# Loading k and v with transposing loads of 256 columns in place of 128, under another written-out order

## The chip, the cores and the metric

The kernel runs on one core of one Trainium2 chip. The metric is the device time of one execution in microseconds (us). Executions can fall into a slower state, so only fast ones are compared. Every execution of the changed kernel and of the variants was of the fast state; of the kernel before, two were slow (318.95 and 317.03 us, in the rounds of e1 to e4 and of e9 to e11) and are left out of every ratio. The one run of e8, another program, is of unknown state. "Times" below are these device times; a profile's "span", from the first to the last instruction, is about 1.7 us shorter.

## The reference

A block with conditioning by six modulation vectors, one sequence of S = 2048 positions, D = 640 channels, bf16:

```python
def _A_ref(q, k, v, shift_k, ssm_k, ssm_D):
    # k_shift: 4-tap causal convolution of k, one filter for each channel
    for t in range(ks):
        k_shift = k_shift + k_pad[:, t:t + S, :] * shift_k[:, ks - 1 - t][None, None, :]
    kv = k_shift * v
    # ... FFT convolution of kv with ssm_k along the sequence (length 2 S) ...
    y = y + kv * ssm_D[None, None, :]
    return q * y
# ...
mod = (_silu(c) @ w_mod).reshape(c.shape[0], 6, 1, -1)       # sa, ca, ga, sb, cb, gb
h = _layernorm(x, axis=-1) * (1 + ca) + sa
x = x + ga * _A_ref(h, A_k, A_v, A_shift_k, A_ssm_k, A_ssm_D)
h = _layernorm(x, axis=-1) * (1 + cb) + sb
x = x + gb * _B_ref(h, B_w1, B_w2, B_w3, B_w4)               # LayerNorm, w1, gelu, shifts, w2, LayerNorm, w3, gelu, w4
```

So k and v are needed early, with channels on the partitions: k is shifted, multiplied with v, and goes into the FFT. The LayerNorms and the four weight matrices of the second part come late.

## The kernel before

Every piece of work is a task with a number. A task knows on which engine it may run, what it reads and writes, and which slots it takes in PSUM, the memory that PE's matmuls write to. The order is not computed: it is written out as a string of task numbers, each with the letter of its engine (S, P, D, A, G for SP, PE, DVE, ACT, POOL) and its PSUM places, and is replayed. Each engine executes its tasks strictly in that order.

```python
CODE = {"P": "PE", "A": "ACT", "D": "DVE", "G": "POOL", "S": "SP"}

def run(self):
    order, seen = [], set()
    for word in ORDER.split():
        head, _, places = word.partition(":")
        t = self.tasks[int(head[:-1])]
        t.on = self.CODE[head[-1]]
        # ... asserts: engine allowed, all dependencies earlier ...
        for sl, place in zip(t.alloc, places):
            sl.place = place
        seen.add(t)
        order.append(t)
    return order
```

The loads that change. A block is 128 channels; there are ND = 5:

```python
for b in range(ND):
    for dst, off, src, key in ((kT, 16, k_flat, "kT"), (vT, 0, v_flat, "vT")):
        add("SP", 3.0, lambda e, b=b, dst=dst, off=off, src=src:
                nc.sync.dma_start_transpose(dst[:, b, off:off + S], src[:, b * P:(b + 1) * P]),
            w=[(key, b, b + 1)], kb=524, rate=200.0)
```

Their users, twice for each block (half a sequence each): PE shifts k by matmuls with diagonal matrices (L456), DVE multiplies with v (L461).

```python
def k_shift(b, s2):
    # PE: four taps, two 512-column halves, into one PSUM slot
    nc.tensor.matmul(pt[:, i, :], lhsT=diagw[:, b, jj, :], rhs=kT[:, b, c0:c0 + 512], start=(jj == 0), stop=(jj == 3))
    # ...
    # DVE: v times the shifted k, in place of v
    nc.vector.tensor_tensor(vs, ps.tile[:].rearrange("p i n -> p (i n)"), vs, ALU.mult)
```

Three late pieces matter to the argument. The statistics of the first LayerNorm, one task of about 1.1 us on DVE for each of 16 tiles (L521 and L522), feed a small finishing task on POOL (L527 to L530):

```python
def ln1_stats(A):
    for i in range(2):
        nc.vector.bn_stats(st[:, i, :], x_all[:, A, i * 320:(i + 1) * 320])
    nc.vector.bn_aggr(mv1[:, A, :], st[:])
```

The other LayerNorms end in `ln_finish`, on DVE or POOL (L667 to L669) and then on POOL (L674 to L676); then `norm` (L557 on ACT, L559 on DVE) scales a tile. And `turn` brings a normalised tile to the transposed form that w1 needs: by PE (L722) and a copy (L728 or L730) for the first three of eight pairs of tiles, by a transposing DMA between two SBUF tiles (L715) for the other five:

```python
pe_tr = (0, 1, 2)

def turn(dT, dk, src, sk, i, g):
    if g not in pe_tr:
        add("SP", 1.3, lambda e: nc.sync.dma_start_transpose(dT[:, :, i * P:(i + 1) * P], src), r=[sk], w=[dk + ("t",)], lat=1.6)
        return
    # ... else five PE transposes into a PSUM slot, then a copy by ACT or DVE ...
```

## Time and profile before

| | kernel before |
|---|---|
| time, median of the 3 runs known at the prediction | 314.69 us (313.75 to 314.99) |
| span of the profiled run | 311.9 us |
| PE, DVE, ACT, POOL busy | 88%, 73%, 63%, 33% |
| bound to some 110 us | DVE (busy 9.3 to 9.9 of each 10 us in 40 to 80 us) and the DMA engines (mean share 0.81 to 1.13 there) |
| bound from some 155 us | PE (busy 29.9 to 30.0 of each 30 us in 170 to 290 us) |

The lines themselves stand in the prediction, with what is to be seen in each. To read them: in a timeline row the first number is the start in us, the second the busy time (for SPq: the time that the issue held SP's queue), then engine, line, operation, output and inputs, and the count of instructions merged in the row. Brackets at the end, where there are any, give the engine's idle time before the row and what ended it.

### The profile page before, as it was taken

What the parts mean: (1) busy time and instruction counts of PE and PEld (TensorE: products, weight loads), DVE (VectorE), ACT (ScalarE), POOL (GpSimd) and SP (SyncE); (2) the same over time, 40 slices, a digit from 0 to 9 for tenths busy, and PEclk for the clock granted to TensorE, in tenths of its full rate; (3) what the DMA queues carried; (4) which work ended last, traced back from release to release, by engine and by line L of the source; (5) the groups of instructions that cost most, each with busy time, mean ns of one, the idle gap of its engine ahead of it and who ended that gap; (6) DMA issues with size and microseconds to landing.
All of it is one profiled execution on the core that took longest, in us unless ns stands there. A gap on an engine that the chain in (4) does not pass through costs nothing.

```text
span 311.9 us, 7129 instructions
## 1 busy us (share of the span) xinstructions
PE 275.1 (88%) x2816; PEld 204.7 (66%) x2816; DVE 228.1 (73%) x460; ACT 197.3 (63%) x314; POOL 101.8 (33%) x227
## 2 busy tenths in 40 slices
PE   0998999999688844778799999999999999999993
PEld 0655656655588632556588787778886768878762
DVE  8999999999999999888976687758744245124233
ACT  4788997889377869879647566766694604342100
POOL 4888227005211416763434331223312103010000
PEclk9999999999789965579999999999999999999998
DMA  5998999997999700820055020221224110320111
GB/s 179 293 184 196 224 182 210 274 226 184 238 253 233 194 9 8 299 92 2 1 128 191 2 58 2 53 49 22 58 61 55 40 41 16 76 53 22 33 47 51
DMA packets 56817, 35.39 MB, mean 113 GB/s; under 512 B 38528, under 2 KB 53504, under 8 KB 56784
## 3 DMA queue, kind: packets, MB, share of 16 engines
q1 hardware_dynamic: 55552, 31.49, 42.6%
q0 software_dynamic: 1136, 3.41, 4.4%
q8 instruction: 22, 0.36, 0.5%
q14 instruction: 11, 0.09, 0.1%
q10 hardware_dynamic: 96, 0.04, 0.1%
HBM read 16.31 MB, written 2.62 MB: 61 GB/s over the span
## 4 chain that ended last, share of the span: by engine, by line
PE 59%; DVE 19%; ACT 8%; POOL 4%; issue 4%; DMA 3%; SPq 0%; DVEq 0%; ACTq 0%; POOLq 0%
PE ps_w L876 18%; PE ps_w L857 17%; PE ps_w L824 5%; DVE Rb L582 5%; PE ps_w L769 4%; PE ps_ksh L456 4%; ACT R L208 3%; PE ps_s L407 2%; PE ps_s L424 2%; DMA Ra<-in_A_ssm_k_dram 2%; PE ps_mod L482 2%; DMA RH<-in_w_mod_dram 2%; DVE R L704 2%; DVE Rb L394 2%; DVE R L461 1%
## 5 line engine op out<-in xcount | busy, mean ns | idle before, releaser
L857 PE MATMUL ps_w<-R,T 128*128 128x256 bf16 x560 | 63.5, 273 | 0.5 <-ACT R L728 0.4
L857 PEld LDWEIGHTS <-T 128*128 128x128 bf16 x560 | 54.4, 98 | 8.3 <-issue 1.6
L876 PE MATMUL ps_w<-T,R 128*128 128x320 bf16 x416 | 59.0, 299 | 0.0
L876 PEld LDWEIGHTS <-R 128*128 128x128 bf16 x416 | 40.6, 98 | 15.4 <-issue 0.3
L861 ACT ACTIVATE R<-ps_w 128x1024 bf16<-128x1024 f32 (+1 forms) x32 | 28.5, 910 | 26.9 <-PE ps_w L857 26.9
L681 ACT ACTIVATE RG<-R 128x640 bf16<-128x640 bf16 x32 | 23.5, 735 | 24.9 <-DVE R L832 18.2
L899 DVE TENSOR_TENSOR T<-ps_w,R 128x640 bf16<-128x640 f32 x15 | 12.3, 823 | 33.6 <-PE ps_w L876 17.2
L208 ACT CAST T<-ps_s 128x1024 bf16<-128x1024 f32 x33 | 31.8, 1018 | 7.4 <-PE ps_s L407 7.2
L407 PE MATMUL ps_s<-F1bd,Rb 128*128 128x256 bf16 x160 | 23.0, 292 | 9.1 <-DVE Rb L394 8.4
L208 ACT CAST R<-ps_s 128x640 bf16<-128x640 f32 x42 | 26.8, 724 | 2.7 <-PE ps_s L424 2.4
L407 PEld LDWEIGHTS <-Rb 128*128 128x128 bf16 x160 | 16.4, 104 | 15.6 <-DVE Rb L394 9.0
L824 PE MATMUL ps_w<-RG,R 128*128 128x320 bf16 x160 | 23.4, 299 | 1.5 <-ACT R L771 1.4
L594 PE MATMUL ps_i<-EB,Rb 128*128 128x128 bf16 x160 | 21.8, 236 | 2.7 <-DVE Rb L582 2.7
L674 POOL TENSOR_TENSOR lnv<-stat,lnv 128x2 f32<-128x2 f32 x24 | 7.0, 290 | 51.7 <-ACT RG L681 44.9
L593 PE MATMUL ps_i<-EA,Rb 128*128 128x128 bf16 x160 | 21.9, 235 | 1.9 <-DVE Rb L582 1.6
L208 ACT CAST T<-ps_i 128x1024 bf16<-128x1024 f32 x18 | 17.2, 1026 | 9.1 <-PE ps_i L594 8.4
L424 PE MATMUL ps_s<-T,RG 64*128 64x320 bf16 x256 | 21.8, 297 | 0.8 <-ACT R L208 0.3
L769 PE MATMUL ps_w<-R,RG 128*128 128x256 bf16 x160 | 21.7, 299 | 0.0
L824 PEld LDWEIGHTS <-R 128*128 128x128 bf16 x160 | 15.2, 98 | 8.1 <-ACT R L771 2.3
L675 POOL TENSOR_TENSOR lnv<-lnv,mhalf 128x2 f32<-128x2 f32 x24 | 19.4, 810 | 1.9
L594 PEld LDWEIGHTS <-Rb 128*128 128x128 bf16 x160 | 16.9, 107 | 4.8 <-DVE Rb L582 4.4
L769 PEld LDWEIGHTS <-RG 128*128 128x128 bf16 x160 | 17.2, 108 | 3.7 <-issue 0.3
(156 smaller groups left out, 502.6 us busy)
## 6 DMA issues: line engine op xcount, KB each, us to landing
RH<-in_w_mod_dram SPq DMA_DIRECT2D x8, 400.0 KB, 5.3
Ra<-in_A_ssm_k_dram SPq DMA_DIRECT2D x5, 512.0 KB, 6.2
Ra<-in_A_q_dram SPq DMA_DIRECT2D x8, 320.0 KB, 6.2
out_dram<-RH SPq DMA_DIRECT2D x60, 40.0 KB, 1.6
T<-in_B_w_dram SPq DMA_DIRECT2D x1, 2160.0 KB, 8.3
T<-in_B_w_dram SPq DMA_DIRECT2D x1, 2080.0 KB, 9.8
RK<-in_w_mod_dram SPq DMA_DIRECT2D x4, 400.0 KB, 4.8
RK<-R SPq DMA_DIRECT2D x5, 256.0 KB, 5.2
```

Source lines behind the costliest of these rows:

```text
L208: nc.scalar.copy(dst, src(ps.tile))
L407: nc.tensor.matmul(psv[:, ml, :], lhsT=xL[:, s0:s0 + P], rhs=F1r, start=True, stop=True)
L424: nc.tensor.matmul(psv[:, g], lhsT=Gs[p, k, 64 - 64 * cc:192 - 64 * cc], rhs=T1b[p, cc * 32 + k], start=(cc == 0), stop=(cc == 1), tile_po ...
L593: nc.tensor.matmul(psv[:, w, :], lhsT=Av[:, r_, :, g_], rhs=EAf, start=True, stop=False)
L594: nc.tensor.matmul(psv[:, w, :], lhsT=Bv[:, r_, :, g_], rhs=EBf, start=False, stop=True)
L675: nc.gpsimd.tensor_tensor(rs, rs, mhalf[:, 0:n], ALU.pow)
L681: add("ACT", 0.74, lambda e: nc.scalar.activation(junk, src, ACT.Square, scale=float(D) ** -0.5, accum_out=stat[:, li, 1, t:t + 1]), r=[sk ...
L769: nc.tensor.matmul(pt[:, fb, :], lhsT=w1_sb[:, b, 160 * fb:160 * fb + P], rhs=hT[:, b, :], start=(b == 0), stop=(b == ND - 1))
L824: nc.tensor.matmul(pt[:, hf, 0:320], lhsT=gsf[:, fb, c0:c0 + P], rhs=w2_sb[:, fb, 320 * hf:320 * hf + 320], start=(fb == 0), stop=(fb == 4))
L857: nc.tensor.matmul(pt[:, fl, :], lhsT=w3_sb[:, b, fb * P:(fb + 1) * P], rhs=xT[:, b, :], start=(b == 0), stop=(b == ND - 1))
L861: nc.scalar.activation(g3[g % 2][:, f0:f0 + fn, :], ps.tile[:, 0:fn, :], ACT.Gelu_apprx_tanh)
L876: nc.tensor.matmul(pts[i][hf][:, hf, 0:320], lhsT=gg[:, fb, i * P:(i + 1) * P], rhs=w4_sb[:, fb, 320 * hf:320 * hf + 320], start=(fb == 0 ...
```

## The change

The intent is fewer and larger loads: four of 1 MiB and two of 512 KiB in place of ten of 512 KiB. The order was written anew to fit (1051 tasks in place of 1055), for the whole kernel, not for its beginning alone.

```diff
 ORDER = """
-19G 0S 18D 20D 21G 23D 22D 24A 56G 27G 29D 28D 25A 2S 31A 30A 36G 37G 68G 69D 26G 90P:0 91A 86P:1 6S 87A 88P:2 89A 4S 72G 73D 104P:3 105A 102P:0
... (the whole string is replaced) ...
+0S 2S 15G 14D 16D 17G 18D 21A 6S 23G 25D 24D 3S 64D 26A 19D 65D 20A 27A 32G 33G 34G 35D 22G 84P:0 36A 5S 85A 82P:1 83A 66G 52G 4S 70G 80P:2 81A 67D
... (the whole string is replaced) ...
 """
@@
-    for b in range(ND):
+    for b, n in ((0, 2), (2, 2), (4, 1)):
         for dst, off, src, key in ((kT, 16, k_flat, "kT"), (vT, 0, v_flat, "vT")):
-            add("SP", 3.0, lambda e, b=b, dst=dst, off=off, src=src: nc.sync.dma_start_transpose(dst[:, b, off:off + S], src[:, b * P:(b + 1) * P]),
-                w=[(key, b, b + 1)], kb=524, rate=200.0)
+            add("SP", 3.0, lambda e, b=b, n=n, dst=dst, off=off, src=src: nc.sync.dma_start_transpose(dst[:, b:b + n, off:off + S], src[:, b * P:(b + n) * P]),
+                w=[(key, b, b + n)], kb=524 * n, rate=200.0)
```

More of the change, by code (lines that the diff above doesn't have):

```diff
@@ L26 @@
 ORDER = """
-19G 0S 18D 20D 21G 23D 22D 24A 56G 27G 29D 28D 25A 2S 31A 30A 36G 37G 68G 69D 26G 90P:0 91A 86P:1 6S 87A 88P:2 89A 4S 72G 73D 104P:3 105A 102P:0
-106P:1 107A 38G 39G 40A 3S 70D 71D 96P:2 97A 98P:3 103D 99A 5S 74G 75D 49G 1S 66G 94P:0 50G 8S 118P:1 9S 114P:2 115A 10S 92P:3 93A 95D 41G 52D 51D 32D
-53A 116P:0 110P:2 119D 84P:3 42G 11S 43G 34S 7S 54A 33G 44A 85A 111A 67D 117D 122P:1 123D 112P:3 113A 108P:2 109A 100P:0 101D 76P:3 77A 203S 45G 47S
-46S 78P:1 79D 35S 82P:2 83A 80P:0 81A 120P:3 170P:1 283D 121D 178P:2 55G 171A 176P:0 179A 180P:1 177A 65G 181D 194P:3 198P:2 195A 199D 234S 48S 202S
@@ L31 @@
-148P:0 57G 58G 200S 149A 142P:1 201S 143D 182P:3 183A 140P:2 141D 231S 12S 13S 144P:0 145A 188P:1 14S 136P:3 15S 189A 137D 162P:2 163A 156P:0 157D
-164P:1 165A 150P:3 151D 190P:2 191A 168P:0 174P:1 175A 169D 196P:3 197A 138P:2 139D 160P:0 161A 16S 186P:1 158P:3 159A 146P:2 184P:0 185A 187D 17S
-166P:1 167A 147D 192P:3 193A 235P:2 236A 152P:0 213D 232P:1 153A 233A 208D 154P:3 155A 172P:2 288P:0 173A 294P:1 295A 289A 284D 126P:3 298P:2 302P:1
-209D 124P:0 214D 59G 60A 299A 303A 210D 296P:2 297A 130P:1 300P:2 301A 127D 125D 290P:3 291A 128P:0 61G 211D 62G 63G 64A 237S 285D 304P:2 306P:3 307A
@@ L35 @@
-131D 134P:1 129D 286D 305A 310P:0 311A 215G 132P:3 312P:2 313A 135D 133D 238P:0 239D 292P:1 293A 314P:3 315A 316P:2 287D 243S 244P:0 245D 240S 318P:1
-317D 319A 326P:3 327D 320P:0 321A 324P:1 325A 322P:2 308P:0 241P:3 212G 393G 246S 247P:1 309A 323D 352P:2 353A 348P:0 242D 248D 486D 380P:3 381A 349D
-252S 253P:1 254D 330P:2 331A 346P:0 347D 338P:3 339A 356P:1 357A 334P:2 335D 392S 390P:0 391A 354P:3 355D 376P:1 362P:2 489D 205S 350P:0 351D 377A
-249S 250P:3 251D 363A 261S 487D 366P:1 367A 255S 382P:2 383D 332P:0 333A 340P:3 341A 262P:1 263A 217D 258S 344P:0 342P:2 343A 328P:3 329A 256P:1 345D
@@ L39 @@
-257D 374P:2 375A 480D 358P:0 276S 359D 364P:3 365A 388P:1 389A 259P:2 260A 275G 281S 481D 279G 277G 264S 368P:0 278G 282G 280G 272S 386P:3 273G 270S
-268S 271G 274G 490D 384P:1 387A 385A 360P:2 369D 378P:0 379A 269S 361D 372P:3 373A 336P:1 370P:2 371A 267S 265P:0 492A 216D 337D 401G 266A 400S 394D
-395D 408S 409G 396P:3 398P:2 399A 493D 491D 402D 494D 397A 403D 410D 404P:1 405A 411D 406P:0 418D 412P:2 413A 417G 414P:3 415A 416S 419D 426D 422P:1
-423A 424S 420P:2 421A 425G 427D 434D 433G 407A 432S 435D 430P:3 431A 428P:1 442D 441G 438P:2 436P:0 437A 440S 443D 446P:3 444P:0 450D 448S 449G 451D
@@ L43 @@
-447A 456S 439A 429A 454P:3 457G 458D 483A 459D 464S 452P:2 466D 460P:1 445A 462P:0 453A 465G 467D 206S 455A 463D 470P:2 471D 461A 207S 468P:3 469A
-488D 495P:01 496A 497A 498P:23 500A 482D 479G 474S 484D 485D 204S 220D 226D 219D 519D 520D 508P:01 218G 499A 543D 522D 523D 524A 544D 477S 525G 521A
-510A 526G 557D 554D 472S 555D 558D 560D 475S 501G 602D 559A 502P:32 509A 556A 545D 546D 503A 531D 527D 532D 528D 504A 529D 530A 561G 533D 535D 511P:10
-534A 505P:32 603D 605D 606D 547D 512A 536G 566A 540D 541P:1 513A 537D 538P:0 562A 563D 542A 539D 478G 221G 564D 551P:1 567D 607A 604A 608G 506A 609G
@@ L47 @@
-568D 565A 569A 570D 552A 610D 611D 517S 612D 571G 572D 575D 549P:0 550A 553G 476S 573P:3 574D 613A 514S 576P:1 577D 586P:0 614D 615D 616D 618D 617A
-619G 587A 584P:3 585A 578D 579D 507A 580D 548D 672D 623D 624P:1 625A 620D 621P:0 622A 473S 591P:3 634P:2 588P:1 675D 676D 677A 673D 678D 592D 674A
-679G 593A 635A 589D 590A 684D 632P:0 518G 633A 636P:3 685D 594G 686D 687A 581D 680D 681D 682D 683A 595G 599D 600P:1 596D 637D 601D 638A 597P:2 639P:0
-598A 656P:3 657A 650P:1 688D 582D 640D 641A 689G 225D 583D 516S 223D 690A 652P:2 691S 740D 642G 643G 644D 692D 693S 647D 648P:0 649D 653A 654P:3 626D
@@ L51 @@
-627D 651A 645P:0 628D 743D 744D 745A 702P:2 700P:1 703A 701A 646D 724P:0 720P:2 741D 742A 227G 746G 704P:1 655A 222D 224G 694D 629D 721A 747G 748D
-695D 229D 705D 707P:3 725A 718P:2 515S 658P:01 630D 708D 709A 749D 706A 710G 711G 631D 715D 712D 752D 719A 753D 754D 750D 756G 755A 806D 660D 716P:3
-717D 713P:2 714A 228D 659P 661D 663S 790P:2 722P:0 786P:3 666D 751A 757G 760A 758A 791A 230G 828D 829D 788P:1 761S 696D 809D 810D 807D 723A 812D 811A
-808A 813G 818D 814A 787A 819D 726P:20 759S 770P:3 815D 816D 697D 789A 728D 768P:1 771A 765D 820D 821A 817A 769A 784P:2 766D 664S 822D 698D 699D 823G
@@ L55 @@
-824A 826D 665S 827S 825S 767D 729D 775P:3 776D 777A 785A 772P:1 773D 778G 774A 667D 727P 833P:3 834A 730S 779G 732S 782A 831P:1 869D 870D 929D 662S
-734D 735D 832A 871A 780D 781S 762A 763D 792P:20 764D 872D 873D 669S 838P:3 737S 839D 731S 874A 739S 830D 835P:1 836D 840A 783S 853P:3 854A 794D 837A
-841D 851P:1 849P:2 793P 847P:3 875G 876G 877D 881A 882D 842G 843A 845A 883D 844S 846S 930D 931A 878D 879D 880A 885G 733S 884A 668S 932D 933D 935D 886G
-887A 888S 850A 800D 801D 802S 907P:0 934A 936G 848A 852A 913P:2 909P:3 941A 889D 908A 942D 943D 671S 944A 890S 893P:1 894A 738S 891P:0 937D 938D 939D
@@ L59 @@
-940A 945D 946G 911P:1 914A 947D 803S 892A 898P:2 899D 910A 948S 949D 950S 670S 895P:0 896D 900A 897A 901D 902G 795D 804S 796S 855P:32 857D 951P:0 952A
-799S 953P:3 798S 856P 863D 736S 858D 954A 959P:0 805S 960D 956P:3 905A 906S 955G 990P:2 991D 993P:0 994D 862S 1041D 912A 915P:12 917D 918D 903A 904S
-974P:0 968P:1 957D 958A 961A 970P:3 969A 797S 864D 865S 972P:1 916P 975A 992A 866S 922S 973A 962G 963G 964D 965S 966D 923D 967S 1004P:0 1005A 995A
-971A 1002P:1 1003A 1006P:2 1007A 861S 976P:03 920S 996G 997G 921S 868S 919S 867S 998D 999S 1000A 978D 1042D 1008P:1 1009A 859S 860S 924D 977P 984D
@@ L63 @@
-1001S 1028P:2 1029A 1030P:0 985D 989S 926S 1024P:1 1031A 987S 1010P:32 986S 988S 979D 983S 980S 1026P:0 925S 927S 1012D 1025A 928S 1013D 1016S 1011P
-1018D 982S 1014S 981S 1019D 1021S 1020S 1023S 1027A 1032P:130 1022S 1035D 1036D 1017S 1015S 1040S 1037S 1033P 1043D 1039S 1044D 1048S 1047S 1038S
-1045S 1034P 1049D 1050D 1053S 1052A 1046S 1051S 1054A
+0S 2S 15G 14D 16D 17G 18D 21A 6S 23G 25D 24D 3S 64D 26A 19D 65D 20A 27A 32G 33G 34G 35D 22G 84P:0 36A 5S 85A 82P:1 83A 66G 52G 4S 70G 80P:2 81A 67D
@@ new lines @@
+94P:3 1S 71D 95A 45G 8S 88P:0 89A 110P:1 68G 111A 69D 108P:2 109D 104P:3 46G 47D 105A 106P:0 107A 9S 86P:1 87D 28D 30S 92P:2 93A 29S 90P:3 91D 98P:0
+37G 38G 39G 40A 41D 43S 42S 100P:1 101A 99A 49A 62G 227S 48D 31G 44S 63D 198S 7S 196S 197S 199S 112P:2 113D 102P:3 96P:1 97A 114P:0 115D 72P:1 103A
+50A 73A 74P:2 230S 75A 78P:3 79D 76P:0 279D 77A 118P:1 119D 176P:2 164P:3 51G 165A 116P:0 117D 177A 188P:3 189A 136P:1 137A 162P:2 163D 170P:3 10S
+171A 172P:0 61G 173D 152P:1 153A 178P:2 179A 150P:3 151D 146P:0 156P:1 157D 147A 154P:2 155A 138P:3 139D 158P:0 166P:1 159A 167D 142P:2 143A 192P:3
@@ new lines @@
+140P:0 190P:1 141A 11S 191A 193D 186P:2 187D 194P:3 195A 180P:0 181D 144P:1 145A 148P:2 149D 134P:3 135A 182P:0 174P:1 184P:2 53G 175A 183A 280D
+231P:3 232A 228P:1 185D 132P:0 229A 133A 160P:3 161D 168P:1 169A 294P:2 295A 209D 389G 207D 54G 292P:0 293A 55G 288P:3 289A 206D 12S 205D 296P:1 297A
+120P:2 210D 290P:0 291A 284P:3 122P:1 204D 285A 13S 123D 56A 239S 121D 298P:0 299A 126P:3 127D 57G 58G 286P:1 124P:0 59G 60A 128P:2 287A 281D 300P:3
+208G 301A 125D 306P:1 307A 129D 130P:0 282D 304P:3 305A 302P:2 303A 233S 234P:1 131D 235D 308P:3 309A 283D 312P:0 313D 314P:2 315A 310P:1 311A 240P:3
@@ new lines @@
+241D 201S 316P:2 317A 318P:1 319A 322P:0 320P:3 321A 323D 482A 236S 237P:2 238D 242S 243P:1 248S 244D 485D 348P:0 349A 386P:2 376P:3 377A 387D 249P:1
+250D 344P:0 372P:2 373D 211G 345A 388S 352P:3 353A 334P:1 335D 350P:0 330P:2 331D 351A 358P:3 359A 342P:1 488D 245S 246P:0 247D 343A 326P:2 327A
+346P:3 347D 328P:1 329A 362P:0 363A 368P:2 369D 324P:3 257S 258P:1 325A 340P:0 213D 251S 259D 254S 336P:2 271S 275G 277S 341A 337A 252P:3 253D 489D
+274G 360P:0 378P:1 361A 260S 278S 370P:2 371A 338P:3 379D 486D 255P:0 264S 263G 256D 339A 476D 267G 366P:2 367A 268S 332P:1 333D 382P:3 265G 266S 269S
@@ new lines @@
+383A 364P:0 365D 270G 380P:2 381A 276S 212D 374P:1 375A 354P:3 355A 272G 384P:2 385A 273S 356P:0 261P:1 262A 357D 390D 391D 396S 397G 404S 394P:3 490D
+477D 483D 392P:2 405G 398D 399D 402P:0 403A 406D 400P:1 395A 407D 410P:0 408P:3 393A 411A 414D 413G 412S 415D 418P:2 422D 419A 401A 416P:0 417A 420S
+421G 423D 424P:2 425A 426P:1 427A 430D 429G 428S 436S 437G 431D 434P:0 435A 438D 439D 432P:2 446D 442P:1 443A 440P:0 409A 444S 445G 447D 448P:1 452S
+441A 454D 450P:3 453G 455D 458P:0 479A 462D 460S 451A 449A 459A 461G 456P:3 463D 466P:1 457A 214G 464P:0 465A 480D 433D 202S 487D 203S 467D 491P:23
@@ new lines @@
+493A 492A 200S 494P:10 496A 495A 478D 221D 216D 215D 481D 518D 519D 520A 515D 516D 517A 504P:32 539D 217G 484D 505A 497G 540D 541D 553D 550D 551D 506A
+521G 472S 522G 552A 554D 556G 468S 527D 528D 555A 598D 523D 599D 524D 525D 498P:01 499A 500A 507P:32 529D 526A 475G 530A 557G 508A 531D 532G 501P:01
+512S 513S 601D 558D 559D 469S 509A 602D 536D 537P:3 538D 604G 533A 534P:2 535D 560D 474G 547P:3 562D 563D 564D 566D 600A 603A 605G 610D 577D 502A 561A
+606A 611D 612D 471S 565A 567G 571D 545P:2 568D 572P:0 573D 548A 470S 569P:3 570D 582P:0 510S 546A 578D 542A 607D 503A 608D 614D 574D 580P:2 543D 609A
@@ new lines @@
+613A 549G 583A 544D 581A 615G 222D 616D 617P:3 619D 219D 620P:1 473S 587P:0 584P:2 621A 618A 630P:1 575D 576D 511S 671D 672D 673A 588D 589A 628P:3
+225D 631A 585D 586A 629A 632P:0 590D 591G 218D 579D 668D 669D 736D 622A 623D 514G 633D 595A 596P:2 592A 593P:1 594D 635P:3 674G 636D 670A 597A 646P:0
+675G 680A 676D 638D 681D 648P:2 634A 624D 739D 637A 639G 647A 682D 683A 223G 643D 644P:1 737D 652P:3 640A 677D 645D 641P:0 678D 684D 649A 653A 642D
+220G 679A 685G 650P:1 651A 740D 741A 720P:2 718P:3 742D 686D 625D 721A 687S 690A 688D 689S 716P:0 738A 743G 224D 719A 696P:1 697A 698P:2 714P:3 699A
@@ new lines @@
+700P:1 691D 692D 805D 744D 693D 694D 748D 749D 715A 745D 746D 750D 626D 751A 752D 701D 747A 703P:2 704D 706D 753G 702A 705A 654P:31 754D 717A 707G
+756D 711D 712P:2 708D 709P:0 710A 713A 226G 655P 627D 806D 807A 695D 656D 757S 755S 766P:0 767A 802D 803D 824A 786P:2 764P:3 808G 865D 804A 784P:0
+787A 662D 825D 657D 765A 768P:1 826D 660S 809G 810D 811D 812D 785A 782P:2 814D 769D 771P:3 722P:01 783A 813A 780P:2 815D 816D 817A 866D 758D 759D 760D
+868D 869D 928D 929D 818G 819G 772D 820D 821S 773A 774D 663D 666S 723P 730D 770A 822A 823S 867A 775G 667S 778D 779S 761A 776D 781A 724D 829P:3 777S
@@ new lines @@
+870A 659S 827P:2 788P:10 871G 872G 873D 830A 877A 878D 874D 875D 828A 664S 658S 879D 880A 881D 831P:3 832D 876A 882G 883A 725D 790D 885D 834P:2 835D
+661S 731D 847P:3 848A 849P:1 850A 930A 886S 762D 763D 789P 665S 833A 925D 837D 836A 838G 841D 884S 889P:2 890A 926D 927A 843P:3 728S 931D 932G 937A
+734S 887P:1 888A 726S 845P:2 844A 839D 840S 842S 909P:1 910A 933D 934D 935D 938D 891P:3 936A 939D 941D 846A 940A 942G 903P:1 904A 894P:2 895D 943A
+944S 727S 796D 945D 733S 896A 905P:1 906A 946S 851P:20 735S 892D 893A 791D 732S 949P:3 950A 947P:1 897G 898G 901A 902S 729S 797D 852P 859D 948A 952P:3
@@ new lines @@
+953D 955P:1 951G 956D 986P:0 989P:3 990D 853D 854D 987D 899A 900S 970P:1 992G 971A 907P:3 908A 968P:2 991A 858S 954A 958D 794S 957A 966P:1 967A 801S
+959G 857S 969A 962D 963S 960D 1037D 961S 911P:03 913D 964P:1 965A 1004P:2 998P:0 856S 988A 795S 912P 1005A 999A 993G 1002P:1 800S 792S 1003A 1000P:2
+972P:01 996D 994A 793S 860D 997S 798S 799S 1001A 914D 974D 915S 919D 995S 1022P:2 1026P:0 973P 916S 1023A 1020P:3 855S 1027A 920D 980D 923S 863S
+1006P:12 918S 924S 1024P:0 1007P 862S 861S 864S 975D 978S 977S 922S 917S 981D 976S 1021A 983S 985S 982S 984S 1025A 921S 1008D 1009D 1010S 1012S 1011S
@@ L66 @@
+1028P:310 1029P 1014D 979S 1015D 1019S 1017S 1031D 1032D 1016S 1018S 1013S 1036S 1033S 1035S 1039D 1030P 1038D 1034S 1040D 1042S 1041S 1043S 1045D
+1046D 1049S 1047S 1048A 1044S 1050A
 """
```

## The prediction

> **What bounds the kernel now.** I read the busy digits of the page first, then the chain that ended last, then the order of time of SP's queue, of PE and of DVE around the k and v loads, and last the table of stretches.
>
> ```profile
> PE 275.1 (88%) x2816; PEld 204.7 (66%) x2816; DVE 228.1 (73%) x460; ACT 197.3 (63%) x314; POOL 101.8 (33%) x227
> ...
> DVE  8999999999999999888976687758744245124233
> ...
> DMA  5998999997999700820055020221224110320111
> ...
> PE 59%; DVE 19%; ACT 8%; POOL 4%; issue 4%; DMA 3%; SPq 0%; DVEq 0%; ACTq 0%; POOLq 0%
> ```
>
> A digit is 7.8 us. There are two halves. Until about 110 us DVE and the DMA engines are both nearly full; after some 155 us the TensorE is full to the end and DVE falls away. The chain gives DMA only 3%, and its two named pieces are the first ssm_k load and one w_mod load. No piece of it is a k or v load. The stretches agree: in 40 to 80 us DVE was busy 9.69, 9.85, 9.48 and 9.31 of each 10 us, and in 170 to 290 us PE was busy 29.98, 30.00, 29.91 and 30.00 of each 30.
>
> SP's queue in order of time (start, time held on the queue) shows the ten loads that change:
>
> ```profile
> 4.56 6.85 SPq L234 DMA_TRANSPOSE R<-in_A_k_dram  x1
> 11.46 2.51 SPq L234 DMA_TRANSPOSE R<-in_A_v_dram  x1
> 14.02 2.48 SPq L234 DMA_TRANSPOSE R<-in_A_k_dram  x1
> 16.54 2.54 SPq L234 DMA_TRANSPOSE R<-in_A_v_dram  x1
> ...
> 31.84 6.34 SPq L234 DMA_TRANSPOSE R<-in_A_k_dram  x1
> 38.23 3.04 SPq L234 DMA_TRANSPOSE R<-in_A_v_dram  x1
> 41.31 2.72 SPq L234 DMA_TRANSPOSE R<-in_A_k_dram  x1
> 44.08 2.51 SPq L234 DMA_TRANSPOSE R<-in_A_v_dram  x1
> 46.63 2.14 SPq L234 DMA_TRANSPOSE R<-in_A_k_dram  x1
> 48.81 3.10 SPq L234 DMA_TRANSPOSE R<-in_A_v_dram  x1
> ```
>
> A transposing load holds the queue about 2.5 us where others take 0.5; the two of over 6 us stand behind a backlog of plain loads. Adding each one's time to landing (the DMA view, stretch by stretch) gives landings at about 14.1, 16.6, 19.2 and 21.2 for k0, v0, k1, v1, and 41.7, 44.1, 46.7, 49.2, 52.0, 54.5 for k2 to v4: one each 2.55 us on average.
>
> Now who uses them, first PE's shifts of k, then DVE's products with v:
>
> ```profile
> 42.31 1.89 PE L456 MATMUL ps_ksh<-R,RQ 128*128 128x512 bf16 x8
> ...
> 47.09 1.89 PE L456 MATMUL ps_ksh<-R,RQ 128*128 128x512 bf16 x8
> ...
> 52.29 1.89 PE L456 MATMUL ps_ksh<-R,RQ 128*128 128x512 bf16 x8
> ```
>
> ```profile
> 45.54 2.54 DVE L461 TENSOR_TENSOR R<-ps_ksh,R 128x1024 bf16<-128x1024 f32 x2
> ...
> 55.08 2.54 DVE L461 TENSOR_TENSOR R<-ps_ksh,R 128x1024 bf16<-128x1024 f32 x2
> ```
>
> No idle time stands before these rows, but they begin 0.6, 0.4 and 0.3 us after k2, k3 and k4 land, and 1.4 and 0.6 us after v2 and v4. The written order is fitted to the landings: other work fills the time, and there is almost no slack.
>
> [...] 524 KB per 2.55 us is 205 GB/s. In short slices of 38 to 52 us it alternates between about 290 GB/s and about 100, so roughly 1.81 us of each period (524/290) is the transfer at full rate and up to 0.74 us looks like a seam. [...]
>
> **The change part by part.** Removed: ten loads of 128 columns. Added: four of 256 and two of 128, the same bytes. Also moved: the order on every engine.
>
> (1) Queue and DMA time. If time goes by bytes alone, a double load holds and transfers for 5.1 us and nothing is gained. If the seam belongs to the instruction, each double load saves 0.74 us, so at most 4 x 0.74 = 3.0 us of the DMA engines, 1.5 of it in the second group. I think half of it is likely.
>
> (2) Landings. Keeping the second group's start, k2 and k3 land together at 43.5 to 44.3 in place of 41.7 and 46.7; v2 and v3 at 48 to 49.3 in place of 44.1 and 49.2; k4 at 50.5 to 52, v4 at 53 to 54.5. The first needed block comes later: k2 by 2 us, v2 by 4 to 5. The last comes up to 1.5 us sooner. In the first group k0 and v0 would come 2 to 4.5 us later, v1 about as now.
>
> (3) The order hides most of that. By task, PE now runs 14 first-stage steps, in place of 9, ahead of the first shift of k, at about 0.69 us each (9 in 14.58 - 8.38): from 8.4 to about 18, while k0 and k1 should be there by about 17. DVE gets its six LayerNorm statistics (1.05 us each, 6.3 us) ahead of the first product of the second group. My sum: DVE's stage-2 copies start about 0.9 us later than 30.2; 12 of 0.78 and one 32x32 transpose of 2.0 bring it to 42.5; the six statistics to 48.8. That is where v2 and v3 land. So neither PE nor DVE should stand idle for long, but the products of block 2 begin at 48.8 instead of 45.5. PE has four PSUM buffers, two of them hold shifted k until then, so I put its last shift at 57.4 in place of 56.2.
>
> (4) Load of the engines. PE keeps its 245 tasks, each with the same matmuls. DVE goes from 316 to 320, ACT 242 to 243, POOL 96 to 89. To the start of the inverse stage DVE gets one subtraction (about 0.5, an estimate from its 128x512 rows), one negation (0.28) and two modulation copies (0.9), and one product of q goes past it (0.36 less); of the copies out of PSUM it has one of 1.17 less and as many of 0.77 as before. Sum about +0.3 us. Part 3's delay is not added in full, since DVE has other work there. I take 0.3 to 1.2 us late at the inverse stage, where DVE is 29.2 of 30 us busy, and this should carry on to the PE-bound half. Its PE work is unchanged, so it shifts as a whole.
>
> (5) 110 to 155 us. PE was idle 11.4 of 30 us in 110 to 140, and the chain hops between DVE, ACT and POOL. The new order has LayerNorm pieces and q tiles in other places here, and a hop more or less is 0.5 to 1 us. I can't sign this: plus or minus 2 us.
>
> Sum: 314.7 + 0.7 (part 4) - 0 (part 1, as no wait on these loads is on the chain) gives 315.4.
>
> **The rivals.** First, the gain of the DMA engines reaches the end: they are full to 110 us, a w_mod load of 4.93 us stands in the chain at 70 us, and 1.5 us saved could pull that load and the q loads forward. Against it: the DMA's part in the chain is 3%, and DVE is full meanwhile. It would give 312 to 313.5. Second, the coarser load becomes a new wait: if a double load takes longer than two, or its output with a stride between blocks runs at a lower rate, PE and DVE stand still at 17 to 23 and 43 to 54 us, since the slack is under 1.5 us. Each us lost there goes to the end, as DVE is full from there on: 318 to 321. Third, the order alone decides: two fitted orders of equal work differ by what part 5 leaves open, 312 to 318, whatever the loads do.
>
> **Range and chances.** Most weight lies with the third, about +0.2%. The second weighs more than the first, for slack is small and gain is off the chain. So 315.4 us, 311.5 to 320.0 for 8 in 10. Under 308.4 would need more than all seams and luck in the order: 0.04. Over 321 needs the coarse load to be slow as well: 0.08. Within 2%: 0.88.
>
> **What would show it.** Step 1: SP's holds of a double load of 4.2 to 5.1 us without backlog, landing spacing the same. Step 2: v2 and v3 landing at 48 to 49.3, k2 and k3 at 43.5 to 44.3. Step 3: no idle over 1 us on PE or DVE with a k or v load as releaser, DVE's first product of the second group near 48.8, PE's last shift near 57.4. Step 4: the first inverse product (L582) 0.3 to 1.2 us after its 79.80 in the kernel before. Step 5: the idle of PE in 110 to 155 us. I would be wrong if a double load's rate differs from 205 to 290 GB/s, if idle with a DMA releaser appears in the first 60 us, or if the tail after 155 us has PE gaps that the kernel before lacks.

## The result and the profile after

The changed kernel took 316.59 us (median of 4 runs, 316.07 to 317.09), the kernel before 314.48 us in the same rounds (4 runs, 313.75 to 314.99). A ratio here and below is the mean time of one kernel's fast runs over the mean of the other's fast runs of the same rounds, so it is not quite the ratio of the medians. It is 1.0069, 95% interval 1.0040 to 1.0098: within 2%, and slower by 0.7%.

The page of the changed kernel, busy time:

```profile
PE 271.5 (86%) x2816; PEld 200.6 (64%) x2816; DVE 227.0 (72%) x470; ACT 199.6 (63%) x315; POOL 104.8 (33%) x214
```

The same number of matmuls, and no engine with much more work. PE and DVE are busy a little less than before (275.1 and 228.1 us), ACT and POOL some 2 and 3 us more (197.3 and 101.8), which is little beside a span of 314.5. What is longer is PE's waiting, and it has to be looked for stretch by stretch. I go along the kernel in order of time.

**The loads.** SP's queue of the changed kernel, the six loads (start, time held):

```profile
4.62 8.02 SPq L234 DMA_TRANSPOSE R<-in_A_k_dram  x1
12.68 4.44 SPq L234 DMA_TRANSPOSE R<-in_A_v_dram  x1
...
27.92 10.11 SPq L234 DMA_TRANSPOSE R<-in_A_k_dram  x1
38.08 4.75 SPq L234 DMA_TRANSPOSE R<-in_A_v_dram  x1
42.87 3.18 SPq L234 DMA_TRANSPOSE R<-in_A_k_dram  x1
46.09 2.60 SPq L234 DMA_TRANSPOSE R<-in_A_v_dram  x1
```

A double load without a backlog holds the queue 4.44 and 4.75 us, less than two single ones of 2.5. (The two of 8.02 and 10.11 were issued behind plain loads, of ssm_k and of q and w_mod, and landed 10.8 and 13.6 us after their issue.) Adding the time from issue to landing: k2 and k3 land at 41.5, v2 and v3 at 46.9, k4 at 48.8, v4 at 50.8, where v4 came at 54.5 before. The last block is in 3.7 us sooner, and the second group was issued 3.9 us sooner, at 27.92 rather than 31.84. In the first group k0 and k1 land at 15.4 and v0 and v1 at 19.1: k0 1.3 and v0 2.5 us later than before, v1 2.1 us sooner.

**Their users.** PE's last shift of k, and DVE's first products of the second group, in the changed kernel:

```profile
53.82 1.89 PE L456 MATMUL ps_ksh<-R,RQ 128*128 128x512 bf16 x8
```

```profile
47.16 3.44 DVE L461 TENSOR_TENSOR R<-ps_ksh,R 128x1024 bf16<-128x1024 f32 x3
```

The products start 0.3 us after v2 and v3 land, the last shift ends at 55.7. No wait of PE or DVE in the first 85 us has a k or v load as its releaser.

**Half way.** The first product of the inverse stage (L582), before and after:

```profile
79.80 1.22 DVE L582 TENSOR_TENSOR Rb<-R,R 128x2048 bf16<-128x2048 bf16 x1
```

```profile
79.52 1.23 DVE L582 TENSOR_TENSOR Rb<-R,R 128x2048 bf16<-128x2048 bf16 x1
```

At 80 us the changed kernel is 0.28 us ahead. The loads and everything around them have cost nothing. At 141 us the two are still level: the third pair's transposes on PE begin at 141.05 before and 141.08 after, and the work that PE then has left to do is the same. In a row of stretches stand the stretch and its length, then the busy time of PE, PE's weight loads, DVE, ACT and POOL, each with its count in brackets, then the granted clock (1.00 is full), the DMA share and GB/s. From the third pair to the end, before and after:

```profile
141.05:312.00 170.95, 163.39 (x1358) 127.70 (x1358) 95.01 (x231) 86.98 (x155) 36.87 (x103) 0.99 0.21 48
```

```profile
141.08:315.00 173.92, 163.38 (x1358) 127.78 (x1358) 94.76 (x239) 88.37 (x156) 35.43 (x91) 0.99 0.17 35
```

The same 1358 matmuls and 163.4 us of PE. In these two profiles the whole difference arises after 141 us.

**Where it is lost.** One row of the stretches of each kernel, 140 to 170 us. First the kernel before, then the changed one:

```profile
140.00:170.00 30.00, 26.88 (x241) 21.75 (x239) 24.31 (x65) 22.08 (x42) 12.99 (x35) 1.00 0.28 84
```

```profile
140.00:170.00 30.00, 24.45 (x221) 20.02 (x222) 25.32 (x74) 23.59 (x43) 12.62 (x29) 1.00 0.07 15
```

PE does 2.43 us less in these 30 us at the same clock. From 170 to 290 us it is busy 99.9% before and 99.6% after, so what it missed is done at the end: in the stretch from 290 us PE has 16.95 us of work before and 19.45 after, 2.50 more. The profiled spans differ by 2.6 us.

PE's waits from 141 us on name the releasers (in all, times, longest, in us). The kernel before, all that the view lists:

```profile
PE ps_w L824 <- ACT R L771: 1.4, 1, 1.4
PE ps_tr L722 <- DVE RK L559: 0.7, 1, 0.7
PE ps_w L857 <- ACT R L728: 0.4, 1, 0.4
PE ps_tr L722 <- DVE RH L559: 0.3, 1, 0.3
PE ps_w1x L779 <- ACT R L728: 0.3, 1, 0.3
```

The changed kernel, likewise:

```profile
PE ps_w L824 <- ACT R L771: 2.4, 1, 2.4
PE ps_tr L722 <- DVE RK L559: 1.3, 1, 1.3
PE ps_tr L722 <- DVE RH L559: 0.8, 1, 0.8
PE ps_w L769 <- DMA R<-RK: 0.7, 1, 0.7
PE ps_tr L722 <- ACT RH L557: 0.6, 2, 0.4
PE ps_w1x L779 <- DMA R<-RK: 0.4, 1, 0.4
```

The waits are for the same kind of thing: LayerNorm tiles that PE needs next. The wait for L559's RK ends at the level point itself and costs nothing: in the changed kernel PE came to it sooner. The others add up to 4.9 us against 2.4, 2.5 more, nearly the difference of the spans (2.6): 1.0 more at L824, 0.7 at L769 for the fourth pair's tiles, transposed by DMA, 0.5 at L722 for RH from DVE, and 0.4 at L779, at 242 us. PE's work still to be done tells the same in order of time: the changed kernel is behind by 0.6 us at 154, by 1.4 at 160, by 2.1 at 170 and by 2.5 at 260. Before 141 us the changed kernel has a wait of 3.5 us (L722 on POOL's L668, until 125.7 us) where the kernel before has one of 3.0 (on ACT's L557). As the two are level afterwards, that one is no part of the loss.

One thing that stands in the way is visible on DVE between 139.2 and 149 us of the changed kernel, the first and the last of four aggregations of LayerNorm statistics for later tiles:

```profile
140.10 0.21 DVE L522 BATCH_NORM_AGGREGATE mv<-ln_st 128x2 f32<-128x12 f32 x1
...
148.60 0.21 DVE L522 BATCH_NORM_AGGREGATE mv<-ln_st 128x2 f32<-128x12 f32 x1
```

Each stands for a task of 1.1 us. The kernel before has none in 130 to 154 us. In 140 to 150 us DVE is busy 8.75 of 10 us before and 9.35 after, PE 7.63 before and 6.53 after.

### The profile page after: what moved, and what is told of

It is laid out like the page before. It is cut to its first block, busy times and chain, and to the rows that moved or that the text cites. A ratio compares the mean times of both kernels' runs of the same rounds, so it can differ in the third digit from the quotient of the medians.

```text
span 314.5 us, 7118 instructions
## 1 busy us (share of the span) xinstructions
PE 271.5 (86%) x2816; PEld 200.6 (64%) x2816; DVE 227.0 (72%) x470; ACT 199.6 (63%) x315; POOL 104.8 (33%) x214
## 2 busy tenths in 40 slices
DMA packets 56721, 35.39 MB, mean 113 GB/s; under 512 B 38400, under 2 KB 53376, under 8 KB 56688
## 4 chain that ended last, share of the span: by engine, by line
PE 60%; DVE 17%; ACT 6%; issue 5%; DMA 4%; POOL 4%; SPq 1%; DVEq 0%; POOLq 0%; ACTq 0%
PE ps_w L876 17%; PE ps_w L857 15%; PE ps_w L824 6%; PE ps_ksh L456 6%; PE ps_s L424 5%; DVE Rb L582 4%; PE ps_s L407 4%; PE ps_w L769 4%; ACT RG L681 3%; PE ps_mod L482 2%; DMA R<-RK 2%; DVE Rb L394 2%; DMA RK<-R 2%; POOL lnv L675 2%; DVE Ra L692 2%
## 5 line engine op out<-in xcount | busy, mean ns | idle before, releaser
L857 PE MATMUL ps_w<-R,T 128*128 128x256 bf16 x560 | 64.4, 273 | 0.0
L876 PE MATMUL ps_w<-T,R 128*128 128x320 bf16 x416 | 59.0, 299 | 0.0
L861 ACT ACTIVATE R<-ps_w 128x1024 bf16<-128x1024 f32 (+1 forms) x32 | 28.9, 913 | 45.4 <-PE ps_w L857 31.1
L876 PEld LDWEIGHTS <-R 128*128 128x128 bf16 x416 | 40.6, 98 | 15.3 <-issue 0.3
L407 PE MATMUL ps_s<-F1bd,Rb 128*128 128x256 bf16 x160 | 21.9, 286 | 10.1 <-DVE Rb L394 9.2
L407 PEld LDWEIGHTS <-Rb 128*128 128x128 bf16 x160 | 15.9, 102 | 16.3 <-DVE Rb L394 10.2
L824 PE MATMUL ps_w<-RG,R 128*128 128x320 bf16 x160 | 23.6, 299 | 2.4 <-ACT R L771 2.4
L832 DVE SCALAR_TENSOR_TENSOR R<-ps_w,R 128x640 bf16<-128x640 f32 x16 | 13.1, 818 | 13.0 <-PE ps_w L824 13.0
L594 PE MATMUL ps_i<-EB,Rb 128*128 128x128 bf16 x160 | 19.2, 220 | 3.7 <-DVE Rb L582 3.7
L593 PE MATMUL ps_i<-EA,Rb 128*128 128x128 bf16 x160 | 19.6, 219 | 2.6 <-DVE Rb L582 1.7
L769 PE MATMUL ps_w<-R,RG 128*128 128x256 bf16 x160 | 20.8, 290 | 0.7 <-DMA R<-RK 0.7
L824 PEld LDWEIGHTS <-R 128*128 128x128 bf16 x160 | 15.4, 98 | 8.4 <-ACT R L771 2.7
L594 PEld LDWEIGHTS <-Rb 128*128 128x128 bf16 x160 | 15.4, 98 | 6.6 <-DVE Rb L582 6.4
```

What stands on the lines that cost most here:

```text
L407: nc.tensor.matmul(psv[:, ml, :], lhsT=xL[:, s0:s0 + P], rhs=F1r, start=True, stop=True)
L593: nc.tensor.matmul(psv[:, w, :], lhsT=Av[:, r_, :, g_], rhs=EAf, start=True, stop=False)
L594: nc.tensor.matmul(psv[:, w, :], lhsT=Bv[:, r_, :, g_], rhs=EBf, start=False, stop=True)
L769: nc.tensor.matmul(pt[:, fb, :], lhsT=w1_sb[:, b, 160 * fb:160 * fb + P], rhs=hT[:, b, :], start=(b == 0), stop=(b == ND - 1))
L824: nc.tensor.matmul(pt[:, hf, 0:320], lhsT=gsf[:, fb, c0:c0 + P], rhs=w2_sb[:, fb, 320 * hf:320 * hf + 320], start=(fb == 0), stop=(fb == 4))
L857: nc.tensor.matmul(pt[:, fl, :], lhsT=w3_sb[:, b, fb * P:(fb + 1) * P], rhs=xT[:, b, :], start=(b == 0), stop=(b == ND - 1))
```

## The experiments

Two questions. Do the wider loads cost or gain, and does the order? And what in the late part loses 2 to 3 us?

| run | loads | order | ratio to before, 95% interval |
|---|---|---|---|
| (changed kernel) | double | new | 1.0069 [1.0040, 1.0098] |
| e1_loads_only | double | old | 1.0043 [1.0021, 1.0065] |
| e2_order_only | single | new | 1.0128 [1.0092, 1.0163] |
| e3_head_new_tail_old | double | new to 80 us, then old | 0.9972 [0.9952, 0.9993] |
| e4_head_old_tail_new | single | old to 80 us, then new | 1.0057 [1.0028, 1.0086] |
| e11_head_new_single_tail_old | single | new to 80 us, then old | 1.0029 [1.0009, 1.0050] |
| e5_cut_at_w1x2 | double | new to 142 us, then old | 1.0088 [1.0057, 1.0119] |
| e6_cut_at_w40 | double | new to 177 us, then old | 1.0191 [1.0155, 1.0226] |
| e7_loads_only_early | double | old, k2 and k3 issued sooner | 1.0254 [1.0225, 1.0283] |
| e9_new_stats_later | double | new, four statistics later | 1.0188 [1.0150, 1.0226] |
| e10_old_stats_sooner | single | old, four statistics sooner | 1.0179 [1.0144, 1.0213] |
| e12_new_stats_after_copy | double | new, as e9, later still | 1.0215 [1.0172, 1.0257] |

e8_loads_alone is another program and has no ratio. All the others give the correct result. Measured against a threshold of 2%, e7 is slower, e6, e9, e10 and e12 are unclear, and the rest are the same; the argument rests on smaller differences, and so on the intervals. e1 to e4, e5 to e8, e9 to e11 and e12 ran on four different chips, each against the kernel before on its own.

### e1_loads_only: the wide loads under the old order

```diff
-    for b in range(ND):
+    for b, n in ((0, 2), (2, 2), (4, 1)):
# and the four loads of the change; in ORDER a double load stands where the first of its two stood
```

> The kernel before with only its loads changed: 256 columns at once, each double load in the place of the first of its pair, every other task in the old order. Theory A (the tail of the new order costs the time, the loads are off the path): ratio to before 0.997 to 1.003, that is 313.5 to 315.5 us, though k2 and v2 now land with k3 and v3. Theory B (the coarser loads cost the 2 us, through the two blocks that wait for each other, and the new order only hides part of it): 316 us or more, with idle of PE or DVE between 42 and 54 us.

Measured: 316.36 us, ratio 1.0043, above the range of theory A. The profiled run was the slowest of the 17 (319.08 us), so its waits show the kind, not the usual size, and that they are all of the 0.43% is not shown. DVE's and PE's waits up to 85 us in this run:

```profile
DVE R L461 <- DMA R<-in_A_v_dram: 3.2, 1, 3.2
```

```profile
PE ps_ksh L456 <- DMA R<-in_A_k_dram: 3.0, 2, 2.1
```

Under the old order the wide load is a new wait, as the second rival of the prediction had it: the first block of a pair came only with the second, and DVE and PE stood there. The double load of v2 and v3 was issued at 40.86 us and landed 7.63 us later, at 48.49, and the product that DVE had waited for began at 48.59. The first inverse product came at 84.1 us. The changed kernel has the same loads and none of these waits, so its order was what removed them.

### e2_order_only: the new order with single loads

```diff
# the new ORDER; each double load in it replaced by its two single loads, one behind the other
     for b in range(ND):
         for dst, off, src, key in ((kT, 16, k_flat, "kT"), (vT, 0, v_flat, "vT")):
```

> The new order with the loads split again into single blocks, the two in the place of one. Theory A: as the changed kernel, ratio to before 1.004 to 1.010 (315.7 to 317.6 us), with the same wait for a transposed block of RK near 169 us. Theory B: 314 to 315 us, as the cause is taken away.

Measured: 318.81 us, ratio 1.0128, above what either theory said. The first inverse product came at 83.4 us. No wait names a k or v load. The single loads left SP's queue at 52.7 us, in place of 48.7 in the changed kernel, and PE waited 1.2 us for a copy between SBUF tiles (RG) and 1.6 us for a piece of w_mod. So under the new order the single loads are the worse ones: from e2 to the changed kernel the double loads are worth 1.0128 / 1.0069, about 0.6%. Neither half of the change is good alone. The order and the width of the loads are fitted to each other.

### e3 and e4: the head of one order with the tail of the other

All tasks up to the first steps of the inverse stage (some 470 of 1051, about 80 us) are the same set in both orders, so the string can be cut there.

```diff
# e3_head_new_tail_old: double loads; ORDER = new[:cut] + old[cut:]
# e4_head_old_tail_new: single loads; ORDER = old[:cut] + new[cut:]
```

> The changed kernel's loads and order up to the first inverse2 step, the kernel before's order from there. Theory A: 313.5 to 314.8 us, since the head was 0.3 to 0.5 us ahead of before at the inverse stage and the tail is the old one. Theory B: 316 us or more, the loss being in the head. If the two orders don't fit at the seam, up to 1 us more for either.

> The reverse: single-block loads and the old order up to the first inverse2 step, the new order from there. Theory A: 316 to 318 us, ratio to before 1.004 to 1.011, with PE short of some 2 us of work in 140 to 170 us. Theory B: 314 to 315 us.

Measured: e3 314.25 us, ratio 0.9972 (22 runs); e4 317.09 us, ratio 1.0057 (8 runs). This is the main result. With the new loads and the new head but the old tail, the kernel is 0.3% faster than before; with the old loads and head and the new tail it is 0.6% slower. The traces agree, and they say where in the tail. From the start of the third pair's transposes on PE (about 141 us) to the end of the span, the kernels with the old tail take 170.9 to 171.7 us (before, e1, e3, e11) and those with the new one 172.8 to 173.4 (the changed kernel, e2, e4). Between the cut and that point the new tail costs nothing: e4 is at it at 140.7 us, the kernel before at 141.05. The wait of L824 on ACT's L771 goes with the tail too: 2.1 to 2.4 us in e2, e4 and the changed kernel, 1.0 to 1.4 in the kernel before, e1, e3 and e11. PE's busy time in 140 to 170 us, which e4's expectation named, can't be used here: it is 26.43 us in e3 and 26.79 in e4, but at a granted clock of 0.94 and not 1.00, and at a lower clock the same work counts as more busy time (20 matmuls of L769 took 2.34 us in the changed kernel at clock 1.00, and 4.42 in e12 at about 0.50).

e3 beats both kernels, by 0.3% and 1.0%.

### e11_head_new_single_tail_old: closing the two by two

```diff
# as e3, with single loads
```

> The fourth corner for the head: new order up to the first inverse2 step with single-block loads, two in the place of one, and the old tail. With double loads this took 0.9972. If orders and loads are fitted to each other: 1.002 to 1.006 (stage 2 late by some us, as in e2). If the load width is indifferent: 0.997 to 0.999.

Measured: 314.53 us, ratio 1.0029, inside the range for orders and loads that are fitted to each other. The first inverse product came at 80.73 us, against 79.45 in e3, the same order with double loads. With the old tail throughout, the head stands at: old order and single loads 1.0000, old and double 1.0043, new and single 1.0029, new and double 0.9972. Each alone loses 0.3 to 0.4%, both together gain 0.3%. The effect of the new tail is then 0.57% on the old head (e4) and 1.0069 / 0.9972, about 0.97% or 3 us, on the new one.

### e8_loads_alone: what the width itself is worth

A kernel that gives a wrong result on purpose: only k's loads, in groups of one, two, four and five blocks, each group waited for before the next.

```diff
+    groups = [[1, 1, 1, 1], [2, 2], [4], [1], [2], [5], [1, 1, 1, 1], [2, 2], [4]]
+    nc.sync.dma_start_transpose(T[:, b:b + w, 16:16 + S], k_flat[:, b * P:(b + w) * P])
```

> Wrong result on purpose: only k's transposing loads, in groups with a wait between them: four of one block, two of two, one of four, one of one, one of two, one of five, then the first three groups again. If the seam belongs to the instruction, the queue is held about 2.5 us by a single load and 4.4 by a double, and four blocks take about 10.0 us from first issue to last landing as four loads, 8.9 as two, 8.3 as one. If time goes by bytes alone: the same for all three.

Measured, SP's queue of this kernel, a single load, a double one and one of five blocks:

```profile
4.81 2.49 SPq L26 DMA_TRANSPOSE T<-in_A_k_dram  x1
...
14.37 4.42 SPq L26 DMA_TRANSPOSE T<-in_A_k_dram  x1
...
42.39 9.44 SPq L26 DMA_TRANSPOSE T<-in_A_k_dram  x1
```

Loads of one, two, four and five blocks by themselves landed 4.3, 6.0, 9.8 and 11.4 us after they were issued: about 1.8 us a block, or 290 GB/s (524 KB in 1.8 us), and some 2.5 us that a load by itself pays once (4.3 - 1.8, or 11.4 - 5 x 1.8). Queued behind each other, single loads landed every 2.5 us and double ones every 3.7 to 3.9, so a pair saves 1.1 to 1.3 us. I had expected at most 0.74. Of the totals for four blocks, which the expectation also named, two can be read, and both were too low: four single loads took 11.9 us from first issue to last landing (10.0 expected), one load of four blocks 9.8 (8.3 expected). The two double loads were issued while the singles were still landing, so their total is not clean. The seam does belong to the instruction. The packets do not grow: the changed kernel moves 38400 packets under 512 B, the kernel before 38528, and all 76400 packets of e8 are under 512 B.

Loads of one, two, four and five blocks held the queue 2.5, 4.4, 7.7 and 9.4 us in e8. As rates, queued loads of 512 KiB come to 205 to 210 GB/s (one per 2.5 us), of 1 MiB to some 270 to 280 (one per 3.7 to 3.9 us). In the kernel before, plain loads of ssm_k moved 410 and 418 GB/s (6 to 8 and 8 to 10 us), the transposing ones some 290 at best.

### e7_loads_only_early: can the old order be helped by issuing sooner?

Under the old order, a copy between SBUF tiles (task 44) held up SP ahead of k2 and k3. It was moved behind the q and w_mod loads that follow.

```diff
# ORDER of e1
- ... 195D 230S 44S ...
+ ... 137D 227S 44S ...
```

> As e1_loads_only, but one small copy that waits for another copy is moved on SP's queue from before the three q loads and one w_mod load to just before the second group of transposing loads, so these four go some 2 to 3 us sooner and the k and v loads of blocks 2 to 4 about 2 us sooner. If the 0.43% of e1 came from PE and DVE waiting for k2/k3 and v2/v3 (3.0 and 3.2 us in its profile): those waits shrink to about 1 us, and the ratio to before is 0.999 to 1.002. If the loads cost in another way (bandwidth taken from other transfers): 1.004 as e1.

Measured: 321.63 us, ratio 1.0254; a miss. The wait that is new among PE's up to 85 us:

```profile
PE ps_s L424 <- DMA RG<-RG: 5.2, 1, 5.2
```

The wait for k shrank as meant, from 3.0 to 0.8 us between the two profiled runs, and that for v from 3.2 to 0.2. But the small copy was now issued behind the q and w_mod loads, took 9.87 us to land (4.3 is the median of such copies in the first 60 us of the kernel before), and its consumer stood for 5.2 us. So this run doesn't say whether the waits for k and v were what e1 lost by. It shows that here, where the DMA engines were full (share 1.08 in 30 to 40 us of e1, the same order but for this copy; e7's own share was not read), moving some transfers ahead made another one late.

### e5 and e6: where in the tail?

```diff
# e5_cut_at_w1x2: ORDER = new up to about 142 us, old behind it
# e6_cut_at_w40: ORDER = new up to about 177 us, old behind it
```

> The changed kernel up to the third first-layer step of the MLP (about 142 us), the old order from there. The kernel with the old order from the inverse2 step on took 0.9972 of before, the changed one 1.0069. If the tail's loss is after 142 us (theory A1: waits between 147 and 170 us for normalised and transposed blocks): 0.996 to 1.000 of before. If it arises between 105 and 142 us (theory A2): 1.004 to 1.008.

> The changed kernel up to its first w4 step (about 177 us), the old order from there. Theory A1: 1.004 to 1.008 of before, as all waits before 170 us are kept. If instead the end of the new order costs it (theory A3, waits after 200 us): 0.998 to 1.001.

Measured: 316.22 us (ratio 1.0088) and 319.44 us (1.0191). Neither place can be cut cleanly: at the seam e5 has a wait of PE at L779 for DVE's L832 of 3.2 us, and e6 one at L876 for ACT's L861 of 2.8 us, which neither parent has. Without the seam e6 would be near the changed kernel, which fits a loss before 177 us, but that is arithmetic and not a measurement. Both ratios lie outside the ranges of their theories, and I count both runs as inconclusive. The traces above answer the first question without them: the profiled kernels are level at 141 us, so theory A2, a loss between 105 and 142 us, does not hold for them.

### e9, e10 and e12: the four statistics

Theory T1: the four statistics that the new tail puts on DVE ahead of the LayerNorm chain are what it loses by. Theory T2: the tail is fitted as a whole, and what is moved by hand only moves the wait. e9 moves the four behind the fourth pair's norm, e10 does the opposite to the kernel before, and e12 moves them behind one more copy.

```diff
# e9_new_stats_later, from the new ORDER
- ... 222D ... 219D ... 225D ... 218D ...   (four statistics) ... 223G ... 220G ...   (their finish on POOL)
+ ... 678D 684D 222D 219D 225D 218D ... 679A 685G 223G 220G ...
# e10_old_stats_sooner, from the old ORDER
+ ... 585A 578D 225D 223D 222D 229D ...     (and taken away from their four later places)
# e12_new_stats_after_copy, from the new ORDER: as e9, with the four statistics a few tasks later
- ... 653A 642D 220G ...
+ ... 653A 642D 222D 219D 225D 218D ...
```

> The changed kernel with four LayerNorm statistics of DVE (tiles 10, 11, 13, 15; 1.05 us each, run between 139 and 149 us) and their two POOL finishes put after the norm of the fourth pair of tiles. Theory T1 (these statistics, drawn ahead, delay the chain of norms that feeds PE between 142 and 170 us): about 2 us less, ratio to before 0.999 to 1.003, PE's idle in 140 to 170 us down from 5.6 to 3 or 4 us. Theory T2 (the loss is spread over the tail, or comes of another part): 1.005 to 1.008, as the changed kernel.

> The reverse in the kernel before, its loads and order else unchanged: the statistics of tiles 10, 11, 12, 15 drawn ahead to where the new order has them. T1: 1.003 to 1.008 of before. T2: 0.998 to 1.002.

> The changed kernel with the four LayerNorm statistics of tiles 13, 11, 15 and 10 moved on DVE behind the fourth pair's norm as in the run before last but one, but now also behind the copy (L730) for which PE then stood 3.2 us; POOL's two dependent finishing steps go behind the fourth pair's scaling. Theory T1 (the statistics drawn ahead of the norm chain are what costs the changed tail its 2 to 3 us): the 2.39 us wait on ACT's L771 falls to about 1.4, no PE wait of over 2 us on L730, PE's busy time in 140 to 170 us goes from 24.45 to 26 or more, and the time is 0.999 to 1.004 of the kernel before. Theory T2 (any shift by hand only moves the wait to the next consumer, as every tail order is fitted as a whole): another wait of 2 us or more appears in 140 to 185 us, PE's busy time there stays under 25.5, and the time is 1.006 or more.

Measured: 320.01 us (1.0188), 319.47 us (1.0179) and 320.87 us (1.0215).

e10 went the way of T1 and much too far: PE's waits on L559 rose from 1.9 to 10.5 us, and in 140 to 145 us PE was busy 1.42 of 5 us. Four statistics in a row ahead of the norm chain do cost (DVE ran them from 137.3 to 141.4 us; in the changed kernel they are spread from 139.2 to 148.8).

e9 and e12 brought the wait of L824 down from 2.4 to 1.4 us, as T1 said. But each got a larger one for it. In e9 (PE's timeline):

```profile
166.31 8.45 PE L857 MATMUL ps_w<-R,T 128*128 128x256 bf16 x50 [3.24 <-DVE R L730]
```

In e12 that wait was gone and the next consumer had it. Pieces of the chain in order of time (start, us, what):

```profile
164.87 0.22 DVE mv L522
...
166.84 0.19 POOL nb L529
...
168.21 2.58 DMA R<-RK
...
170.93 1.22 PE ps_w L769 x5
```

The four statistics now stand at 161 to 165 us, exactly ahead of the norms of the fourth pair, whose scale POOL had ready at 162.3. Between those two norms comes one of q, which needs POOL's finish of a statistic; then the DMA transposes, and PE waits 3.6 us at L769 where it waited 0.7. In the changed kernel the same chain was held by POOL: it had the finishing steps of the statistics in 158.8 to 163.6 us ahead of the pair's own.

What PE then loses is more than the wait. Stretches of e12:

```profile
170.00:175.00 5.00, 4.07 (x20) 2.84 (x21) 4.51 (x11) 0.00 (x0) 0.86 (x2) 0.50 0.05 9
175.00:180.00 5.00, 5.00 (x37) 3.86 (x36) 1.01 (x6) 3.61 (x7) 0.00 (x0) 0.82 0.00 0
```

The granted clock was 0.50 and 0.82 after the gap of 3.62 us, and 1.00 in the 5 us before. In other runs the clock, in the 5 us in which a wait of PE ended and in the next 5, was 0.53 and 0.79 in e9 (wait of 3.24 us), 1.00 and 1.00 in e5 (3.25 us), 0.91 and 0.75 in e6 (2.38 us), 1.00 and 1.00 in the changed kernel (2.39 us). In e4 it was 0.66 in 150 to 155 us, after a wait of 2.1 us. So waits of the same length cost clock in some of these runs and none in others; what decides it is not shown.

An estimate from these rows: 4.07 x 0.50 + 5.00 x 0.18 = 2.9 us lost to the clock, if the work done goes with the clock (the 20 matmuls of L769 took 4.42 us here and 2.34 at 1.00). The wait at L769 is 3.6 - 0.7 = 2.9 us longer and that at L824 1.0 us shorter, so there is 1.9 us more of waiting; together 4.8 us. By the ratios e12 lies 1.0215 / 1.0069, 1.45% or 4.6 us, above the changed kernel.

So in e9 and e12 the wait moved on, as T2 said, and T1 is right on a single link: the statistics do lengthen one wait by 1.0 us. Taking them away from there does not bring the time back, because in the new tail there is no free place for 4.4 us of DVE that I found. The times of e9 and e10 lie above the ranges of both theories.

## Why the prediction was right

The time (315.4 predicted, 316.59 measured) and the class were right, and the range held. Its steps fared differently.

**Step 1 (seam).** Right, and the part thought half likely is what e8 shows: holds of 4.44 and 4.75 us in the changed kernel, 4.42 in e8. The term was sized too small: 1.1 to 1.3 us for each pair (e8) against 0.74. As said, nothing of it reached the end by itself: with the old order it was worth less than nothing (e1).

**Step 2 (landings).** The order of events was right, the times 1.1 to 3.7 us too late. That both blocks of a double load come together, which the step took for granted, is what e1 showed (landed at 48.49, used from 48.59). The step began with "Keeping the second group's start"; that failed, as it moved from 31.84 to 27.92. In the first group k0 was later by less than the 2 to 4.5 us named, and v1, said to land as now, was 2.1 us sooner.

**Step 3 (the order hides the coarser release).** Right where it counts: no idle for a k or v load. The two times named were too late, 47.16 in place of 48.8 and 55.7 in place of 57.4, since they were built on step 2.

**Step 4 ("0.3 to 1.2 us late at the inverse stage").** This failed. The changed kernel was 0.28 us early there, and e3 shows that this head is worth -0.28% of the time. My sum added work to DVE and left out what earlier loads give back: under this head double loads bring the first inverse product from 80.73 (e11) to 79.45 us (e3) and the time from 1.0029 to 0.9972. The sum was also added up wrongly: its own items come to +0.15 us, not +0.3. The predicted +0.7 us has the sign of the measured +2.1 only because another term, which I could not sign and put at zero, had it. That is luck.

**Step 5 (the late order, unsigned, plus or minus 2 us).** This is where the time went, about 3 us on the new head (e3 against the changed kernel), more than the 2 us allowed for, and later than the 110 to 155 us named: in the profiles 0.6 of 2.5 us had been lost at 154 us and 2.1 at 170. The prediction said that it would be wrong if the tail after 155 us had PE gaps that the kernel before lacks. It has them: 0.76 us at 158.5 and 0.72 us at 168.7, where the kernel before has none.

**The rivals.** The third, that the order alone decides, is the one that held for the sign. The second, a new wait for the coarse load, is real under the old order (e1, +0.43%). The first, a gain of the loads, is real only under an order made for them, 0.6% (from e2 to the changed kernel, and from e11 to e3). Against the kernel before, head and loads together gain 0.28%, 0.9 us, and not the 1.2 to 2.7 us that this rival gave.

**What stays open.** That the loss lies in the order behind 80 us is shown by e3 and e4; that it arises after 141 us, and at which waits, was read in the profiled runs. What makes each of these waits longer is argued from the chains and not shown: e5 and e6 were spoiled at their seams, and e9, e10 and e12 changed more than they took away. The next try would be to put the four statistics behind the fourth pair's DMA transposes and take the q norm between its two norms along; it was not run. Nor do I know why the new tail costs 0.97% on the new head and 0.57% on the old one; the intervals nearly cover the difference.

## What to carry to other kernels

When a change alters a transfer and the order together, try each alone and cut the order in two: here the half that the change was about gained 0.3%, and an unrelated half of the same rewrite lost three times as much. A wider load saved a fixed part for each instruction (1.1 to 1.3 us for a pair of queued loads, e8), but released its first block as late as its last (DVE's wait of 3.2 us in e1), so here it paid only with an order refitted to that. And after a refit, look at the waits of the whole kernel, as work that is free on its own engine (here 1.1 us of statistics on DVE, or its finish on POOL) may stand ahead of the one chain that the bounding engine is waiting for.
